# Strassen products for the paired first layers of batches 2 and 3, in an attention-plus-two-MLPs kernel on one Trainium2 core

## The chip, the cores and the metric

One core of one Trainium2 chip. The metric is the device time of one execution in microseconds (us), measured without the profiler; 1371.0 us is the median of three runs before the change. The profile is one further execution, taken with the hardware profiler on; its times are its own. Engines: PE is TensorE (matmuls; PEld are its weight loads), ACT is ScalarE, DVE is VectorE, POOL is GpSimd, SP issues most DMAs.

## The reference

Batch 4, 12 heads, sequence 448, head size 64, so a model width of 768. Attention with capped scores, then an MLP over a normalised input, then a second block that mixes tokens and has an MLP of its own:

```python
scores = cap * np.tanh(scale * q @ k.T / cap); attn = softmax(scores); x = attn @ v     # (4, 448, 768)
xn = (x - mean) / np.sqrt(var + 1e-06) * g_ln
x = x + np.maximum(xn @ w_ch1, 0.0) @ w_ch2                   # w_ch1 768 x 3072: "MLP 1"
u = x + (np.maximum(x.T @ w_tok1, 0.0) @ w_tok2).T            # token mixing, per batch
out = u + np.maximum(u @ w_ch1, 0.0) @ w_ch2                  # w_ch1 768 x 1536: "MLP 2"
```

All data is float32. Each matrix operand is kept as a high and a low part, and a product takes three matmul passes (high-high, low-high, high-low).

## The kernel before

Work is written down as steps; a planner (`Program.emit`) puts the steps of each engine in one fixed order by a key (roughly the time at which a step is due) and by its own estimates of cost. The chip then runs these orders, with semaphores between the engines. So a change in what is written, or in a key, can move any instruction behind it.

Both MLPs are cut into groups of 512 hidden units: six groups in MLP 1 (`NG1`), three in MLP 2 (`NG2`). A group (`mlp`) has a first layer of four row tiles (128 hidden units each) and a second layer of six output tiles. For one batch a first-layer tile is 6 x 3 = 18 matmuls of 128 x 448 (L587) into one PSUM bank; ACT rectifies the bank into the high part (L592) and DVE makes the low part (L593). A second-layer tile is 4 x 3 = 12 matmuls (L608), and DVE adds the bank to the residual `x` (L612). So one group costs one batch 72 + 72 = 144 matmuls. The planner takes a first-layer tile in three parts and a second-layer tile in two, so work of another kind can stand between the parts.

A group runs "paired", for two batches on the same weights, or "solo". Weights were split into high and low parts at first use and kept in DRAM; later uses load them (L296) into three rotating buffers `split`. The last third of the program handles batches 2 and 3:

```python
weave(mlp(groups((2,), 0, n1)))                     # n1 = 6: MLP 1 of batch 2, solo
layer_norm(3)
normalise(3)
weave(mlp(groups((2, 3), n1, NG1 - n1)))            # none, as n1 = NG1
weave(tokens(2, HIDDEN[2]), mlp(groups((3,), 0, n1)), ahead=TOKENS_AHEAD)
weave(tokens(3, HIDDEN[2]), mlp(groups((2,), NG1, n2)), ahead=TOKENS_AHEAD)
weave(mlp(groups((2, 3), NG1 + n2, NG2 - n2), (2,)))
weave(mlp(groups((3,), NG1, n2), (3,)))             # n2 = 2
```

So 16 of the 17 late group runs are solo and one is paired. PSUM has four separate tiles `bank0` to `bank3` of 512 columns, and two tiles `sc0` and `sc1` of two times 512 columns each, which attention uses for its scores, both halves at a time. The MLPs take their banks from a ring; behind attention that ring holds `bank1` to `bank3`.

Of the kernel before, what the change touches and what calls it, by code (L numbers as in the profile page):

```python
# [9 lines left out]
F32 = mybir.dt.float32  # L10
# [9 lines left out]
C = H * D  # L20
# [5 lines left out]
G = 4  # L26
# [60 lines left out]
class Program:  # L87
# [1 line left out]

    FIXED = {"pe": 0.0, "act": 0.19, "dve": 0.08, "pool": 0.15, "dma": 0.3}
    RATE = {"pe": 203e-3 / S, "act": 0.83e-3, "dve": 1.14e-3, "pool": 2.4e-3, "dma": 2.9e-3}
    LATER = {"dma": 3.31}

    def __init__(self):
# [55 lines left out]
def block_kernel(ctx: ExitStack, tc: tile.TileContext, qkv, cap, gln, w1, w2, wt1, wt2, con, out):  # L152
# [10 lines left out]
    def place(name, shape, dtype=F32):  # L163
        return cp.tile([P, *shape], dtype, name=name)

    def boxes(name, n, shape, dtype=F32):
        return [Box(place(f"{name}{i}", shape, dtype)) for i in range(n)]
# [32 lines left out]
    HID = boxes("h", 2 * G, [2, S], F32R)  # L200


    area_t = place("area", [4 * S + QKV + 5 * S])
    ends = [0]

    def area(n):
        ends.append(ends[-1] + n)
        return area_t[:, ends[-2]:ends[-1]]

    own_t = area(4 * S).rearrange("p (e s) -> p e s", e=4)  # L210
# [3 lines left out]
    QK, V = [Box(area(S + 4 * P))], [Box(area(4 * DV).rearrange("p (c d) -> p c d", c=4))]  # L214
    two = [Box(area(S)), Box(area(S))]
    SQ = [Box(area(S))]
    SUM, OTHER = [Box(area(S))], [Box(area(S))]
    TWICE = [Box(OTHER[0].at[:, :CC].rearrange("p (e a d) -> p e a d", e=3, a=2), OTHER)]
    QS, KS = boxes("qs", 1, [2, S], F32R), boxes("ks", 1, [4 * P], F32R)

    VS = boxes("vs", 1, [4, DV + D], F32R)
    EH, EL = boxes("eh", 1, [2, S], F32R), boxes("el", 1, [2, S], F32R)
    M, N = boxes("m", 2, [2, 2, NJ]), boxes("n", 1, [2, 2, NJ])
    rs_t, rm_t = [place(f"rs{i}", [H, NJ]) for i in range(2)], [place(f"rm{i}", [H, NJ]) for i in range(2)]
    RS = [[Box(t[:, 6 * g:6 * g + 6]) for g in range(2)] for t in rs_t]
    RM = [[Box(t[:, 6 * g:6 * g + 6]) for g in range(2)] for t in rm_t]
    R, VA = boxes("r", 1, [2, 32]), boxes("va", 1, [3, 8])
    MEAN, RSTD = boxes("mean", 1, [S]), boxes("rstd", 1, [S])

    BANKS = [Box(pp.tile([P, 512], F32, name=f"bank{i}")) for i in range(4)]  # L230
    SC = [Box(pp.tile([P, 2, 512], F32, name=f"sc{i}")) for i in range(2)]

    def ring(of):
        while True:
            yield from of


    GL, PAIR = Box(gl), Box(pair_r)

# [314 lines left out]
        prog.key += cols * prog.RATE["pe"] * stretch  # L554

    n_tile = 0

    def prepare(g):

# [9 lines left out]
    def mlp(plan, ends=()):  # L569

        nonlocal n_tile
        for n_group, (g, bs) in enumerate(plan):
            final = [b for b in bs if all(b not in o for _, o in plan[n_group + 1:])]
            hid = {b: [] for b in bs}
            hidden = HIDDEN[len(bs) == 1]
            for i in range(G):
                no, row = n_tile, g * G + i
                n_tile += 1
                load(no, w1, row, C)
                w = split_t[no % 3]  # L580
                for b in bs:
                    ph, ht, src = next(main_banks), next(hidden), BIG[b % 2]
                    for part in range(3):
                        def product(part=part, w=w, src=src, ph=ph):
                            for cc in (2 * part, 2 * part + 1):
                                for n, (wi, xi) in enumerate(PASSES):
                                    mm(ph.at[:, :S], w[:, wi, cc * P:(cc + 1) * P], src[cc].at[:, xi],  # L587
                                       start=(cc, n) == (0, 0), stop=(cc, n) == (NCC - 1, 2))

                        need = SPLIT[no % 3][:1] if part == 0 else SPLIT[no % 3][1:] if part == 2 else SPLIT[no % 3]  # L590
                        pe(6 * S, product, [*need, src[2 * part], src[2 * part + 1]], [ph])
                    add("act", S, lambda ht=ht, ph=ph: act(ht.at[:, 0], ph.at[:, :S], AF.Relu), [ph], [ht], early=EVACUATE)  # L592
                    add("dve", S, lambda ht=ht, ph=ph: dve.scalar_tensor_tensor(  # L593
                        ht.at[:, 1], ph.at[:, :S], 0.0, ht.at[:, 0].bitcast(F32), op0=ALU.max, op1=ALU.subtract), [ph], [ht], early=EVACUATE)
                    hid[b].append(ht)
                    yield
            for e in range(NCC):
                no, row = n_tile, g * NCC + e
                n_tile += 1
                load(no, w2, row, G * P)  # L600
                w = split_t[no % 3]
                for b in bs:
                    py, x = next(main_banks), X[b][e]
                    for part in range(2):
                        def product(part=part, w=w, h=hid[b], py=py):
                            for i in (2 * part, 2 * part + 1):
                                for n, (wi, hi) in enumerate(PASSES):
                                    mm(py.at[:, :S], w[:, wi, i * P:(i + 1) * P], h[i].at[:, hi],  # L608
                                       start=(i, n) == (0, 0), stop=(i, n) == (G - 1, 2))

                        pe(6 * S, product, [*SPLIT[no % 3], hid[b][2 * part], hid[b][2 * part + 1]], [py])
                    add("dve", S, lambda x=x, py=py: dve.tensor_tensor(x.at, x.at, py.at[:, :S], op=ALU.add), [py], [x], early=EVACUATE)  # L612
                    if b in ends and b in final:
                        add("dma", S // 2, lambda b=b, e=e, x=x: nc.sync.dma_start(out=out[e, :, b], in_=x.at), [x], ())
                    yield
            if mixing and len(bs) == 2 and n_group >= 1:
                prog.key -= LEAD
                piece(*mixing.pop(0))
                prog.key += LEAD
# [182 lines left out]
```

## Time and profile before

| | |
|---|---|
| runs without the profiler | 1371.0, 1377.17, 1370.46 us, median 1371.0 |
| profiled execution: span from first to last instruction | 4738.7 us (the page gives no other time of this execution) |
| PE busy in it | 4729.0 us, 100% |
| DVE, ACT, POOL busy | 897.2, 624.6, 88.9 us |
| granted TensorE clock, mean | 1.000 (the upper level, 2.4 GHz) |

The profiled execution takes 3.456 times the median of the runs. A busy time is the sum of the instructions' own durations; an engine that is 100% busy leaves no idle time in which another engine's lateness would show.

### The profile page before, as it was taken

Reading aid. Unit: us, or ns where it says so; the run is one execution under the profiler, and the core shown is the slowest. Engines: PE = TensorE matmul, PEld = TensorE weight load, DVE = VectorE, ACT = ScalarE, POOL = GpSimd, SP = SyncE. Lnnn points to the kernel's source line nnn. Section 1 sums busy time; section 2 is a strip of 40 time slices with the busy share of each in tenths; the row PEclk is TensorE's granted clock in tenths of the full one; section 3 lists DMA queues with packets and bytes.
Section 4 is the critical chain, followed back from the end, with each engine's and each line's share of the span. In section 5 each row is a group of like instructions: output and inputs, shape, how many; then the busy total and the mean of one; then the engine's idle time right before and its main releaser. Section 6 shows DMA issues by size and latency. Waiting matters only on the chain.

```text
span 4738.7 us, 17824 instructions
## 1 busy us (share of the span) xinstructions
PE 4729.0 (100%) x6468; PEld 2684.3 (57%) x6468; DVE 897.2 (19%) x1612; ACT 624.6 (13%) x1006; POOL 88.9 (2%) x79
## 2 busy tenths in 40 slices
PE   9999999999999999999999999999999999999999
PEld 2223555555655556665555555555656555656555
DVE  2231222222222222222222221100000000000000
ACT  3321111211121111121111110000000000000000
POOL 1100000000000000000000000000000000000000
DMA  3221122111212111221111211111111111111111
GB/s 105 97 66 39 46 69 67 59 61 64 67 55 67 63 57 41 67 65 61 60 60 51 72 57 53 57 62 58 53 53 44 61 59 60 51 47 42 37 57 58
DMA packets 147095, 281.04 MB, mean 59 GB/s; under 512 B 10816, under 2 KB 79680, under 8 KB 147008
## 3 DMA queue, kind: packets, MB, share of 16 engines
q1 hardware_dynamic: 146432, 279.62, 18.5%
q8 instruction: 51, 0.84, 0.1%
q10 hardware_dynamic: 576, 0.29, 0.0%
q14 instruction: 36, 0.29, 0.0%
HBM read 217.74 MB, written 62.13 MB: 59 GB/s over the span
## 4 chain that ended last, share of the span: by engine, by line
PE 100%; DMA 0%; ACT 0%; DVE 0%; issue 0%
PE bank L587 39%; PE bank L608 39%; PE bank L384 6%; PE sc L363 3%; PE sc L366 3%; PE bank L408 3%; PE bank L663 2%; PE bank L685 2%; PE bank L639 1%; PE bank L466 1%; PE bank L531 0%; PE bank L495 0%; PE bank L511 0%; DMA area<-in_qkv 0%; PE bank L445 0%; PE bank L444 0%
## 5 line engine op out<-in xcount | busy, mean ns | idle before, releaser
L587 PE MATMUL bank<-big,split 128*128 128x448 f32 x2592 | 1898.7, 995 | 1.1 <-ACT big L543 1.1
L608 PE MATMUL bank<-h,split 128*128 128x448 f32 x2592 | 1896.3, 995 | 0.0
L587 PEld LDWEIGHTS bank<-big,split 128*128 128x128 f32 x2592 | 1109.4, 429 | 750.5 <-issue 740.4
L608 PEld LDWEIGHTS bank<-h,split 128*128 128x128 f32 x2592 | 1109.5, 428 | 744.9 <-issue 741.6
L612 DVE TENSOR_TENSOR x<-x,bank 128x448 f32<-128x448 f32 x216 | 134.1, 621 | 1407.4 <-PE bank L608 1407.4
L592 ACT ACTIVATE h<-bank 128x448 fp32r<-128x448 f32 x144 | 78.4, 545 | 1817.5 <-PE bank L587 1817.5
L593 DVE SCALAR_TENSOR_TENSOR h<-bank,h 128x448 fp32r<-128x448 f32 x144 | 89.9, 624 | 1182.2 <-ACT h L592 1182.1
L366 PE MATMUL sc<-qs,ks 128*128 128x448 f32 x192 | 151.5, 994 | 0.0
L384 PE MATMUL bank<-x,area 128*96 128x448 f32 (+1 forms) x88 | 129.3, 1665 | 0.0
L363 PE MATMUL sc<-area 64*128 64x448 f32 x112 | 112.0, 1695 | 5.0 <-DMA area<-in_qkv 5.0
L366 PEld LDWEIGHTS sc<-qs,ks 128*128 128x128 f32 x192 | 82.5, 431 | 57.6 <-issue 57.2
L384 PE MATMUL bank<-x,x 128*96 128x448 f32 (+1 forms) x76 | 112.5, 1675 | 0.0
L685 PE MATMUL bank<-t,h 128*128 128x448 f32 x144 | 108.3, 996 | 0.0
L176 ACT ACTIVATE split<-whole 128x384 fp32r<-128x384 f32 (+1 forms) x96 | 54.0, 564 | 340.2 <-PE bank L608 228.7
L276 ACT ACTIVATE whole<-raw 128x384 f32<-128x384 f32 (+2 forms) x130 | 76.7, 593 | 125.5 <-DVE split L172 107.8
L663 PE MATMUL bank<-big,t 128*128 128x384 f32 x136 | 89.8, 899 | 0.0
L172 DVE TENSOR_TENSOR split<-whole,split 128x384 fp32r<-128x384 f32 (+1 forms) x112 | 68.9, 619 | 108.1 <-ACT split L176 107.7
L408 PE MATMUL bank<-el,vs 128*128 128x448 f32 x96 | 88.6, 989 | 0.0
L685 PEld LDWEIGHTS bank<-t,h 128*128 128x128 f32 x144 | 61.4, 427 | 40.8 <-issue 40.0
L384 PEld LDWEIGHTS bank<-x,area 128*96 128x96 f32 (+1 forms) x88 | 28.5, 347 | 95.4 <-issue 85.5
L279 DVE SCALAR_TENSOR_TENSOR whole<-raw,whole 128x384 int32<-128x384 int32 (+2 forms) x130 | 79.8, 616 | 0.2
L363 PE MATMUL sc<-x 64*128 64x448 f32 x80 | 79.4, 1692 | 0.0
(112 smaller groups left out, 1719.0 us busy)
## 6 DMA issues: line engine op xcount, KB each, us to landing
split<-kept SPq DMA_DIRECT2D x160, 384.0 KB, 3.4
split<-kept SPq DMA_DIRECT2D x120, 512.0 KB, 3.6
raw<-in_w SPq DMA_DIRECT2D x72, 384.0 KB, 3.3
kept<-split SPq DMA_DIRECT2D x72, 384.0 KB, 3.0
raw<-in_w SPq DMA_DIRECT2D x54, 512.0 KB, 3.6
kept<-split SPq DMA_DIRECT2D x54, 512.0 KB, 3.3
area<-in_qkv SPq DMA_DIRECT2D x38, 480.0 KB, 3.5
area<-in_qkv SPq DMA_DIRECT2D x35, 192.0 KB, 2.4
```

Of the source, the lines that this page charges most:

```text
L279: add("dve+", m, lambda: dve.scalar_tensor_tensor(f, hi, -(1 << 31), f, op0=ALU.bitwise_and, op1=ALU.bitwise_or), [r], [w])
L363: mm(sc.at[:, i, :S], k[rows, c * P:(c + 1) * P], q[rows], start=True, stop=True)
L366: mm(sc.at[:, i, :S], ks.at[:, c * P:(c + 1) * P], qs.at[:, j], start=j == 0, stop=j == 1)
L384: mm(po.at[:DV, :S], v.at[:n, c], E[c // 2][0][:n, c % 2], start=c == 0, stop=c == 3)
L408: mm(po.at[:, :S], vs.at[:, c, :P], part.at[:, i], start=c == 0 and part is eh, stop=c == 3)
L587: mm(ph.at[:, :S], w[:, wi, cc * P:(cc + 1) * P], src[cc].at[:, xi], start=(cc, n) == (0, 0), stop=(cc, n) == (NCC - 1, 2))
L592: add("act", S, lambda ht=ht, ph=ph: act(ht.at[:, 0], ph.at[:, :S], AF.Relu), [ph], [ht], early=EVACUATE)
L593: add("dve", S, lambda ht=ht, ph=ph: dve.scalar_tensor_tensor(ht.at[:, 1], ph.at[:, :S], 0.0, ht.at[:, 0].bitcast(F32), op0=ALU.max, op1=A ...
L608: mm(py.at[:, :S], w[:, wi, i * P:(i + 1) * P], h[i].at[:, hi], start=(i, n) == (0, 0), stop=(i, n) == (G - 1, 2))
L612: add("dve", S, lambda x=x, py=py: dve.tensor_tensor(x.at, x.at, py.at[:, :S], op=ALU.add), [py], [x], early=EVACUATE)
L663: mm(pj.at[:, :CC], t1[:, wi, sc * DT + j * P:sc * DT + (j + 1) * P], cols(xs[sc])[:, xi], start=(sc, wi, xi) == (0, 0, 0), stop=(sc, wi) ...
L685: mm(pu.at[:, :S], hT[j].at[:, hi, a:a + P], t2[:, wi, j * S:(j + 1) * S], start=(j, n) == (0, 0), stop=(j, n) == (1, 2))
```

## The change

In a group that is paired for batches 2 and 3, the first layer is computed as Strassen products. The 2 x 2 blocks are: weights, two row tiles by two halves of the width 768; inputs, two halves of the width by two batches. A quad (`quads`, two per group) makes two row tiles for both batches from seven block products of nine matmuls (`times`), where eight such blocks of work stood before. The sums of input blocks `X1` to `X4` are made once per MLP by `sides`, the sums of weight blocks for each quad by `weights`; every sum is split into high and low part by ACT and DVE. DVE adds the products (`plus`) into `TMP` buffers, from which `rectify` makes the hidden tiles. `relay` places the new buffers on tiles that attention and the splitting of weights no longer need. The constants change the division into groups: MLP 1 of batch 2 now runs 3 groups solo, batch 3 runs 1 + 2 solo, 3 are paired; in MLP 2 each batch runs 1 solo and 2 are paired. That is 8 solo and 5 paired group runs. From this point on the ring of banks has eight entries, the four halves of `sc0` and `sc1` and then the four banks.

```diff
-N0, N1, N20, N2 = 1, 6, 1, 2
+N0, N1, N20, N2, N30 = 1, 3, 1, 1, 1
+QUAD_LEAD, SIDES_LATER, SIDES_PACE = 16.0, 20.0, 4.0
...
-    SC = [Box(pp.tile([P, 2, 512], F32, name=f"sc{i}")) for i in range(2)]
+    sc_t = [pp.tile([P, 2, 512], F32, name=f"sc{i}") for i in range(2)]
+    SCB = [Box(t[:, i]) for t in sc_t for i in range(2)]
+    SC = [Box(t, SCB[2 * i:2 * i + 2]) for i, t in enumerate(sc_t)]
...
+    def split(to, src, cols):
+        add("act/dve*+", cols, lambda e: copy(e, to.at[:, 0], src.at), [src], [to])
+        add("dve+", cols, lambda: low(dve, to.at[:, 1], src.at, to.at[:, 0]), [src], [to])
+
+    def join(to, pair, cols):
+        add("dve+/pool+", cols, lambda e: engine_of[e].tensor_tensor(
+            to.at, pair.at[:, 0].bitcast(F32), pair.at[:, 1].bitcast(F32), op=ALU.add), [pair], [to])
+
+    def both(to, a, b, op, cols):
+        add("dve+", cols, lambda: dve.tensor_tensor(to.at, a.at, b.at, op=op), [a, b], [to])
...
+            join(f21, a21, CC)
+            join(f22, a22, CC)
+            both(f22, f21, f22, ALU.add, CC)
+            split(s1, f22, CC)
+            join(f11, a11, CC)
+            both(f21, f11, f21, ALU.subtract, CC)
+            both(f11, f22, f11, ALU.subtract, CC)
+            split(s2, f11, CC)
+            split(a21, f21, CC)
+            join(f12, a12, CC)
+            both(f12, f12, f11, ALU.subtract, CC)
+            split(s4, f12, CC)
...
+        def times(w, x):
+            bank = next(main_banks)
+
+            def product():
+                for c in range(3):
+                    for n, (wi, xi) in enumerate(PASSES):
+                        mm(bank.at[:, :S], w.at[:, wi, c * P:(c + 1) * P], x[c].at[:, xi],
+                           start=(c, n) == (0, 0), stop=(c, n) == (2, 2))
+
+            pe(9 * S, product, [w, *x], [bank])
+            return bank
...
+            p5 = times(s1, X1)
+            p6 = times(s2, X2)
+            plus(c21, p6, c11)
+            plus(c11, p2, c11)
+            h11 = rectify(2, c11)
+            plus(c12, p5, c21)
+            p7 = times(s3, X3)
+            plus(c22, p7, c12)
+            plus(c21, p7, c21)
+            p4 = times(a22, X4)
+            plus(c21, p4, c21)
...
+            if bs == (2, 3):
+                yield from quads(g, hid, hidden)
-            for i in range(G):
+            for i in range(G if bs != (2, 3) else 0):
...
+        main_banks = ring(SCB + BANKS)
+        relay()
+        sides(SIDES_LATER)
+        weave(mlp(groups((3,), 0, N30)))
         weave(mlp(groups((2, 3), n1, NG1 - n1)))
-        weave(tokens(2, HIDDEN[2]), mlp(groups((3,), 0, n1)), ahead=TOKENS_AHEAD)
+        weave(tokens(2, HIDDEN[2]), mlp(groups((3,), N30, n1 - N30)), ahead=TOKENS_AHEAD)
         weave(tokens(3, HIDDEN[2]), mlp(groups((2,), NG1, n2)), ahead=TOKENS_AHEAD)
-        weave(mlp(groups((2, 3), NG1 + n2, NG2 - n2), (2,)))
-        weave(mlp(groups((3,), NG1, n2), (3,)))
+        sides(SIDES_LATER)
+        weave(mlp(groups((3,), NG1, n2)))
+        weave(mlp(groups((2, 3), NG1 + n2, NG2 - n2), (2, 3)))
```

What this does to the orders shows at two places. The first is PE in the second layer of a paired group. Before (the paired group of MLP 2), a tile of batch 2 reads the hidden tiles `h0`, `h2`, `h4`, `h6`, a tile of batch 3 the odd ones, each in a bank of its own; a row's last bracket names the semaphores (DMA queues or engines) that the instruction waits for.

```order
L608 MATMUL bank1_112<-h0_86,split1_78 128x448 [waits DMAHW4_49,DVE_49]
L608 MATMUL bank1_112<-h0_86,split1_78 128x448 x2
L608 MATMUL bank1_112<-h2_88,split1_78 128x448 x3
L608 MATMUL bank1_112<-h4_90,split1_78 128x448 x3
L608 MATMUL bank1_112<-h6_92,split1_78 128x448 x3
L608 MATMUL bank2_113<-h1_87,split1_78 128x448 [waits DVE_49]
L608 MATMUL bank2_113<-h1_87,split1_78 128x448 x2
L608 MATMUL bank2_113<-h3_89,split1_78 128x448 x3
L608 MATMUL bank2_113<-h5_91,split1_78 128x448 x3
L608 MATMUL bank2_113<-h7_93,split1_78 128x448 x3
```

After (first paired group of MLP 1; L770 is the same line, batch 2 reads `h0`, `h1`, `h4`, `h5`), both tiles of one `split` buffer stand in `sc0`: twelve matmuls in its first half, then twelve in its second half.

```order
L770 MATMUL sc0_117<-h0_86,split2_79 128x448 [waits DMAHW0_49]
L770 MATMUL sc0_117<-h0_86,split2_79 128x448 x2
L770 MATMUL sc0_117<-h1_87,split2_79 128x448 x3
L770 MATMUL sc0_117<-h4_90,split2_79 128x448 x3
L770 MATMUL sc0_117<-h5_91,split2_79 128x448 x3
L770 MATMUL sc0_117<-h3_89,split2_79 128x448 x3
L770 MATMUL sc0_117<-h2_88,split2_79 128x448 x3
L770 MATMUL sc0_117<-h7_93,split2_79 128x448 [waits DVE_49]
L770 MATMUL sc0_117<-h7_93,split2_79 128x448 x2
L770 MATMUL sc0_117<-h6_92,split2_79 128x448 x3
```

What moved is a wait. Before, a tile waits at its start, for DVE to have read what stood in the same bank three tiles earlier. After, the second part of the tile in the second half waits for DVE. The awaited instruction is the addition of `sc0`'s first half to `x2`, and that addition waits for PE's first six matmuls into the second half. DVE's order at this place (L774 is L612 of before, L609 is `join`, L613 is `both`):

```order
L774 TENSOR_TENSOR x2_82<-x2_82,bank2_115 128x448 [waits PE_49]
L774 TENSOR_TENSOR x3_83<-x3_83,bank3_116 128x448 [waits PE_49]
L774 TENSOR_TENSOR x2_82<-x2_82,sc0_117 128x448 [waits PE_49]
L774 TENSOR_TENSOR x3_83<-x3_83,sc0_117 128x448 [waits PE_49]
L609 TENSOR_TENSOR late_pair_6982<-split1_78 128x384 [waits DMAHW7_49,DMAHW3_49]
L613 TENSOR_TENSOR v_96<-late_pair_6982,v_96 128x384 [waits DVE_49,Pool_49]
L774 TENSOR_TENSOR x2_82<-x2_82,sc1_118 128x448 [waits PE_49]
```

Here the weight sums of the next quad (L609, L613) have moved between the additions of the second layer.

The second place is PE in the first layer. Before, a row tile takes 18 matmuls for batch 2 (`big0`) and 18 for batch 3 (`big1`):

```order
L587 MATMUL bank2_113<-big0_84,split0_77 128x448 [waits DMAHW0_49]
L587 MATMUL bank2_113<-big0_84,split0_77 128x448 x8
L587 MATMUL bank2_113<-big0_84,split0_77 128x448 [waits DMAHW1_49]
L587 MATMUL bank2_113<-big0_84,split0_77 128x448 x8
L587 MATMUL bank3_114<-big1_85,split0_77 128x448 [waits DVE_49]
L587 MATMUL bank3_114<-big1_85,split0_77 128x448 x17
```

After, products of nine matmuls follow each other, and those on sums (`late_...`, `ksvs`, `eh0`) wait for ACT and DVE, which made the sums:

```order
L673 MATMUL bank3_116<-late_x1_6262,late_qk_6984 128x448 [waits Activation_49]
L673 MATMUL bank3_116<-late_x1_6262,late_qk_6984 128x448 [waits DVE_49]
L673 MATMUL bank3_116<-late_x1_6262,late_qk_6984 128x448 x7
L673 MATMUL sc1_118<-big1_85,ksvs_102 128x448 [waits Activation_49]
L673 MATMUL sc1_118<-big1_85,ksvs_102 128x448 [waits DVE_49]
L673 MATMUL sc1_118<-big1_85,ksvs_102 128x448 x7
L673 MATMUL sc1_118<-big0_84,split0_77 128x448 [waits DMAHW6_49]
L673 MATMUL sc1_118<-big0_84,split0_77 128x448 x8
```

What moved is that the weights no longer come from a DMA alone; sums made on DVE, POOL and ACT stand between the DMA and PE.

## Rows read from the trace of the kernel before

**Rows 1.** The page: span; busy us (share of the span) and instructions per engine.

```profile
span 4738.7 us, 17824 instructions
...
PE 4729.0 (100%) x6468; PEld 2684.3 (57%) x6468; DVE 897.2 (19%) x1612; ACT 624.6 (13%) x1006; POOL 88.9 (2%) x79
```

**Rows 2.** The page: the chain that ended last, shares of the span.

```profile
PE 100%; DMA 0%; ACT 0%; DVE 0%; issue 0%
```

**Rows 3.** Waits on PE, whole span: engine, line, releaser: us in total, times, longest.

```profile
PE sc L363 <- DMA area<-in_qkv: 5.0, 1, 5.0
PE bank L587 <- ACT big L543: 1.1, 1, 1.1
```

**Rows 4.** Chain in order of time, 3000 to 3400 us: start, us, what.

```profile
3056.92 51.67 PE bank L587 x72
3108.59 51.67 PE bank L608 x72
```

**Rows 5.** Stretches of the last part: us, busy per engine (instructions), clock, DMA share, GB/s.

```profile
core 0: us, PE busy (x) PEld busy (x) DVE busy (x) ACT busy (x) POOL busy (x), PEclk, DMA share, GB/s
2500.00:3000.00 500.00, 500.00 (x702) 298.13 (x701) 118.66 (x205) 63.93 (x92) 9.06 (x7) 1.00 0.18 57
3000.00:3500.00 500.00, 500.00 (x711) 299.56 (x710) 34.94 (x57) 15.11 (x29) 0.00 (x0) 1.00 0.19 59
4000.00:4500.00 500.00, 500.00 (x715) 300.72 (x714) 40.80 (x67) 19.01 (x36) 0.00 (x0) 1.00 0.14 45
```

**Rows 6.** Instructions in order of time, 3000 to 3030 us: start, us, engine, line, operation.

```profile
3004.78 26.15 PE L608 MATMUL bank<-h,split 128*128 128x448 f32 x36
...
3005.19 0.55 ACT L592 ACTIVATE h<-bank 128x448 fp32r<-128x448 f32 x1 [10.51 <-PE bank L587]
...
3005.77 0.62 DVE L593 SCALAR_TENSOR_TENSOR h<-bank,h 128x448 fp32r<-128x448 f32 x1 [10.43 <-ACT h L592]
...
3013.80 0.62 DVE L612 TENSOR_TENSOR x<-x,bank 128x448 f32<-128x448 f32 x1 [7.40 <-PE bank L608]
...
3022.46 0.62 DVE L612 TENSOR_TENSOR x<-x,bank 128x448 f32<-128x448 f32 x1 [8.04 <-PE bank L608]
```

**Rows 7.** Instructions in order of time, 570 to 600 us.

```profile
584.10 1.96 ACT L543 ACTIVATE big<-area 128x448 fp32r<-128x448 f32 x4
...
584.72 8.87 PE L587 MATMUL bank<-big,split 128*128 128x448 f32 x12 [1.10 <-ACT big L543]
```

**Rows 8.** Groups by line and shape, DVE, ACT, POOL: busy us, mean ns of one, idle before.

```profile
L612 DVE TENSOR_TENSOR x<-x,bank 128x448 f32<-128x448 f32 x216 | 134.1, 621 | 1407.4 <-PE bank L608 1407.4
L484 DVE TENSOR_TENSOR area<-x,mean 128x448 f32<-128x448 f32 x36 | 21.2, 618 | 20.6 <-ACT mean L496 20.6
L172 DVE TENSOR_TENSOR split<-whole,split 128x384 fp32r<-128x384 f32 x64 | 36.0, 569 | 56.6 <-ACT split L176 56.6
L176 ACT ACTIVATE split<-whole 128x384 fp32r<-128x384 f32 x55 | 28.3, 518 | 108.6 <-PE bank L608 47.9 <-issue 45.5 <-DVE whole L280 15.1
L543 ACT ACTIVATE big<-area 128x448 fp32r<-128x448 f32 x24 | 12.6, 568 | 32.6 <-DVE area L541 32.6
L172 POOL TENSOR_TENSOR split<-whole,split 128x384 fp32r<-128x384 f32 x8 | 8.0, 1005 | 44.1 <-ACT split L176 24.1 <-DVE split L178 20.0
```

**Rows 9.** The page: DMA queue of SP, and issues (KB each, us to landing).

```profile
q1 hardware_dynamic: 146432, 279.62, 18.5%
...
split<-kept SPq DMA_DIRECT2D x160, 384.0 KB, 3.4
split<-kept SPq DMA_DIRECT2D x120, 512.0 KB, 3.6
```

More of the change, by code (lines that the diff above doesn't have):

```diff
@@ L161, in block_kernel, with place @@
     dp = ctx.enter_context(tc.tile_pool(name="dp", bufs=1, space=bass.MemoryType.DRAM))
-    def place(name, shape, dtype=F32):
-        return cp.tile([P, *shape], dtype, name=name)
+    def place(name, shape, dtype=F32, tag=""):
+        return cp.tile([P, *shape], dtype, name=name, tag=tag or name)
     def boxes(name, n, shape, dtype=F32):
@@ L200, in block_kernel @@
     HID = boxes("h", 2 * G, [2, S], F32R)
[L203 to L210, printed above, removed]
+    own_t = place("own", [4, S])
     own = [Box(own_t[:, i]) for i in range(4)]
@@ L213, in block_kernel @@
     OWN = [Box(own_t[:, 2 * i:2 * i + 2], own[2 * i:2 * i + 2]) for i in range(2)]
[L214 to L217, printed above, removed]
+    QK = boxes("qk", 1, [S + 4 * P])
+    v_t, two_t = place("v", [4 * DV]), place("two", [2, S])
+    V = [Box(v_t.rearrange("p (c d) -> p c d", c=4))]
+    two = [Box(two_t[:, i]) for i in range(2)]
+    SQ, SUM, OTHER = boxes("sq", 1, [S]), boxes("sum", 1, [S]), boxes("other", 1, [S])
     TWICE = [Box(OTHER[0].at[:, :CC].rearrange("p (e a d) -> p e a d", e=3, a=2), OTHER)]
-    QS, KS = boxes("qs", 1, [2, S], F32R), boxes("ks", 1, [4 * P], F32R)
-    VS = boxes("vs", 1, [4, DV + D], F32R)
+    QS = boxes("qs", 1, [2, S], F32R)
+    ksvs_t = place("ksvs", [4 * P + 4 * (DV + D)], F32R)
+    KS, VS = [Box(ksvs_t[:, :4 * P])], [Box(ksvs_t[:, 4 * P:].rearrange("p (c d) -> p c d", c=4))]
     EH, EL = boxes("eh", 1, [2, S], F32R), boxes("el", 1, [2, S], F32R)
     M, N = boxes("m", 2, [2, 2, NJ]), boxes("n", 1, [2, 2, NJ])
-    rs_t, rm_t = [place(f"rs{i}", [H, NJ]) for i in range(2)], [place(f"rm{i}", [H, NJ]) for i in range(2)]
+    r_t = place("rsm", [4 * H * NJ])
+    rs_t, rm_t = [[r_t[:, i * H * NJ:(i + 1) * H * NJ].rearrange("p (h j) -> p h j", h=H) for i in two_of] for two_of in ((0, 1), (2, 3))]
     RS = [[Box(t[:, 6 * g:6 * g + 6]) for g in range(2)] for t in rs_t]
@@ L235, in ring, with halves_of, relay, later @@
             yield from of
+    X1, X2, X3, X4 = LATE = [[Box(), Box(), Box()] for _ in range(4)]
+    WF, WS = [Box() for _ in range(4)], [Box() for _ in range(3)]
+    TMP = [Box(r_t[:, :S], [box for of in RS + RM for box in of]), *SQ, *SUM, *OTHER, *MEAN, *RSTD]
+    def halves_of(t):
+        return t.rearrange("p (a s) -> p a s", a=2)
+    def relay():
+        def later(old, boxes, fill):
+            old = [p for box in old for p in box.parts]
+            add("place", 0, fill, (), old + boxes)
+        def fill_x(b):
+            t = place(f"late_x{b}", [3, 2, S], F32R, tag=f"x{b}")
+            for i in range(3):
+                LATE[b][i].at = t[:, i]
+        for b in range(2):
+            later(X[b], LATE[b], lambda b=b: fill_x(b))
+        def fill_raw():
+            for i in range(3):
+                X3[i].at = place(f"late_raw{i}", [2, S], F32R, tag=f"raw{i}")
+            X4[2].at = QS[0].at
+        later(RAW + QS, [*X3, X4[2]], fill_raw)
+        def fill_own():
+            t = place("late_own", [2, 2, S], F32R, tag="own")
+            for i in range(2):
+                X4[i].at = t[:, i]
+        later(own, X4[:2], fill_own)
+        def fill_weights():
+            for i in range(2):
+                WF[i].at = place(f"late_whole{i}", [CC], tag=f"whole{i}")
+            WF[2].at = place("late_pair", [CC], tag="pair_r")
+            WF[3].at = v_t
+            WS[0].at = halves_of(place("late_two", [2 * CC], F32R, tag="two"))
+            WS[1].at = halves_of(place("late_qk", [2 * CC], F32R, tag="qk0"))
+            WS[2].at = halves_of(ksvs_t[:, :2 * CC])
+        later([*WHOLE, PAIR, *V, *two, *QK, *KS, *VS], [*WF, *WS], fill_weights)
+        for box in (*EH, *EL):
+            WS.append(Box(box.at[:, :, :CC], [box]))
     GL, PAIR = Box(gl), Box(pair_r)
@@ new lines, in sides @@
+    def sides(later):
+        t0 = prog.key
+        for c in range(3):
+            prog.key = t0 + later + c * SIDES_PACE
+            f12, f22, f11, f21 = (next(tmps) for _ in range(4))
+            for to, pair in ((f11, BIG[0][c]), (f12, BIG[1][c]), (f22, BIG[1][c + 3]), (f21, BIG[0][c + 3])):
+                join(to, pair, S)
+            both(f11, f12, f11, ALU.subtract, S)
+            split(X1[c], f11, S)
+            both(f12, f22, f12, ALU.subtract, S)
+            split(X3[c], f12, S)
+            both(f22, f22, f11, ALU.subtract, S)
+            split(X2[c], f22, S)
+            both(f21, f21, f22, ALU.subtract, S)
+            split(X4[c], f21, S)
+        prog.key = t0
@@ new lines, in quads, with weights, plus, rectify @@
+    def quads(g, hid, hidden):
+        nonlocal n_tile
+        pieces = []
+        s = [split_t[(n_tile + k) % 3] for k in range(3)]
+        sb = [SPLIT[(n_tile + k) % 3] for k in range(3)]
+        halves = [Box(s[k][:, :, i * CC:(i + 1) * CC], [sb[k][i]]) for k in range(3) for i in range(2)]
+        n_tile += 3
+        def weights(q):
+            a21, a22, a11, a12 = halves[:4] if q == 0 else WS[3:] + halves[4:]
+            row = g * G + 2 * q
+            t0 = prog.key
+            prog.key = t0 - QUAD_LEAD
+            for box, r, at in ((a22, row + 1, CC), (a21, row + 1, 0), (a11, row, 0), (a12, row, CC)):
+                kb = kept[C, r, at]
+                add("dma", CC, lambda box=box, kb=kb: nc.sync.dma_start(out=box.at.bitcast(F32), in_=kb.at), [kb], [box])
+            f11, f12, f21, f22 = WF
+            s1, s2, s4 = WS[:3]
+            join(f21, a21, CC)
[10 more added lines that the diff above has]
+            split(s4, f12, CC)
+            prog.key = t0
+            return a11, a12, a22, s1, s2, a21, s4
+        def times(w, x):
+            bank = next(main_banks)
+            def product():
+                for c in range(3):
+                    for n, (wi, xi) in enumerate(PASSES):
[3 more added lines that the diff above has]
+            return bank
+        def plus(to, bank, t):
+            add("dve", S, lambda: dve.tensor_tensor(to.at, bank.at[:, :S], t.at, op=ALU.add), [bank, t], [to])
+        def rectify(b, src):
+            ht = next(hidden)
+            add("act", S, lambda: act(ht.at[:, 0], src.at, AF.Relu), [src], [ht], early=EVACUATE)
+            add("dve+", S, lambda: dve.scalar_tensor_tensor(
+                ht.at[:, 1], src.at, 0.0, ht.at[:, 0].bitcast(F32), op0=ALU.max, op1=ALU.subtract), [src], [ht], early=EVACUATE)
+            return ht
+        b11, b21, b22 = BIG[0][:3], BIG[0][3:], BIG[1][3:]
+        for q in range(2):
+            a11, a12, a22, s1, s2, s3, s4 = weights(q)
+            c11, c21, c12, c22 = (next(tmps) for _ in range(4))
+            p1 = times(a11, b11)
+            add("act", S, lambda c11=c11, p1=p1: act(c11.at, p1.at[:, :S], AF.Copy), [p1], [c11])
+            p2 = times(a12, b21)
+            yield
+            p5 = times(s1, X1)
[9 more added lines that the diff above has]
+            plus(c21, p4, c21)
+            h21 = rectify(2, c21)
+            h22 = rectify(3, c22)
+            yield
+            p3 = times(s4, b22)
+            plus(c12, p3, c12)
+            h12 = rectify(3, c12)
+            hid[2] += [h11, h21]
+            hid[3] += [h12, h22]
+            yield
```

5 lines of the change are left out of this document (3 added, 2 removed).

## The prediction

> **What bounds the kernel now.** I read the page's engine line first [rows 1], then the chain that ended last [rows 2], then PE's waits [rows 3]. PE is busy for 4729.0 of 4738.7 us, the whole chain is PE, and in all PE waited twice, 5.0 us for the first load and 1.1 us for ACT. So in the profiled execution the time is the number of matmuls times their pitch. In the pure MLP stretch, 72 matmuls take 51.67 us [rows 4], a pitch of 717.6 ns. The granted clock is 1.00 in every stretch that I read [rows 5], which is the upper level, and both idle times left it there.
>
> The profiled execution is no scale model of a run: a run takes 1371.0 us. If all but the two idle times (6.1 us) shrinks alike, the factor is (1371.0 - 6.1) / (4738.7 - 6.1) = 0.2884, and a matmul has a pitch of 207 ns in a run. That is a ceiling. If a twentieth of the run were idle time that the profile's slow PE hides, the pitch would be 197 ns. What ACT, DVE and a DMA take is a duration in its own right, and I use it unscaled. So everything beside PE weighs 3.5 times as much in a run as the page shows: DVE's 897.2 us [rows 1] are 19% of the span but 65% of a run. I make the sum in the profiled time and in the run's time, and the forecast is for the run. About 0.5% (6.9 us, 1364.1 to 1377.9) is what a measurement of this kernel can tell from no change.
>
> **What the change removes.** Two first-layer row tiles for two batches are eight blocks of nine matmuls; a quad makes seven products. Five paired groups with two quads each save 10 x 9 = 90 matmuls. All else on PE keeps its count. In the profiled time that is 90 x 0.7176 = 64.6 us, in a run 90 x 0.207 = 18.6 us (17.7 at the pitch of 197 ns).
>
> It also removes loads: 13 late group runs in place of 17, four times eight 384 KB and six 512 KB loads. PE waited for no such load [rows 3], so I cost that at nothing. The cover in a run: a solo second-layer tile takes 12 x 0.207 = 2.48 us; with three buffers a load has two tiles, 4.97 us, and needs 3.6 us to land [rows 9] behind 0.41 us from the last matmul (below). Some 0.9 us are to spare.
>
> **What it adds beside PE.** Per quad DVE gets seven additions out of PSUM and four low parts at 0.62 us, four sums and four low parts of weights at 0.57 us [rows 8]: 11.4 us. POOL gets up to four joins at 1.0 us. PE needs 63 x 0.207 = 13.0 us for the quad. Behind two quads stands their group's second layer, 144 x 0.207 = 29.8 us of PE, in which DVE has only 12 additions, 7.4 us. So a paired group is 2 x 13.0 + 29.8 = 55.9 us of PE, 30.2 us of DVE and 8 us of POOL. The weight sums are due 16 us ahead (`QUAD_LEAD`) and stand among the second layer's additions in DVE's order, as the change's part shows. `sides` is 12 times join, sum and split on each of two occasions: at most 36 x 0.62 = 22 us of DVE beside a solo group of 29.8 us. I cost all this at nothing. If the cover were gone, it would be the second rival below.
>
> At this place the trace and a rule of the Trainium skill have to be weighed. The row: POOL's subtraction of 384 columns takes 1005 ns over eight instances and DVE's 569 ns [rows 8]; none of these rows shows one engine blocked by the other for a whole instruction. The Trainium skill, page "SBUF — State Buffer", section "Who interferes with whom", says that a DVE instruction with two SBUF inputs and a GpSimd instruction that reads SBUF exclude each other, and that the later one blocks until the first is done. By that rule the joins would come on top of DVE's time; by the row they run beside it. No run here shows which.
>
> **What it adds on PE: waits.** This decides. The ring now begins with the four halves of `sc0` and `sc1`, and the built program treats the two halves of one `sc` as one tile. DVE's addition of the first half waits for PE's first part into the second half, and the second part waits for that addition. Before, the ring held three tiles, and the wait at a tile's start was for the reader of the tile three back; it cost nothing [rows 3].
>
> The price of one such wait, from the last matmul before it to the next: PE to DVE, 12 matmuls from 3004.78 us at 0.7176 end at 3013.39, DVE starts at 3013.80 [rows 6], 0.41 us; the addition, 0.62 us; to PE, the first L543 ends at 584.10 + 0.57 = 584.67 [rows 7, 8] and PE, which waited for it, starts at 584.72, 0.05 us. Together 1.08 us. It does not shrink with PE. Through ACT alone, at 0.55 us [rows 6], it is 1.01 us; through ACT and then DVE, with 0.03 us between them [rows 6], 1.66 us.
>
> Counted along the changed order, with the awaited instructions: 13 second-layer tiles and two transposes between their parts wait for an addition with nothing to cover it, 15 x 1.08 = 16.2 us; solo first-layer tiles wait five times, twice for ACT, twice for DVE behind ACT, once for both, 2 x 1.01 + 2 x 1.08 + 1.66 = 5.8 us; three more waits are partly covered by other matmuls, together between nothing and 3.2 us, and I take 1.0. In quads the same dependency only delays DVE: a product is one step of nine matmuls, so no part of it waits. The sum is 23.0 us. Bounds: DVE's 0.62 us alone for 20 waits, 12.4 us; and 20 times 1.08 plus one more addition queued ahead on DVE, 0.62, plus 3.2, 37 us. I take 23.0, since rows 6 show DVE idle when such an addition comes.
>
> **Sum.** Profiled: 4738.7 - 64.6 + 23.0 = 4697.1 us. Run: 1371.0 - 18.6 + 23.0 = 1375.4 us. The Strassen saving is real and the waits eat it.
>
> **Rivals.**
> *The waits are cheap.* PE's weight loads run ahead of matmuls, and PEld is busy for only 57% [rows 1]; if PE and DVE overlapped more of the chain than I think, the price would fall towards DVE's 0.62 us or nothing. For it: the drain of 0.41 us is read in an execution whose matmuls are slow. Against: the awaited addition reads the very bank whose matmuls must have drained, and PE started only 0.05 us behind ACT's end in the one such case. Time: 1371.0 - 18.6 + 12.4 = 1364.8 us, and 1352.4 us if they cost nothing. It counts as faster from 0.58 us per wait.
>
> *The operands of the quads come late: slower.* Place: the first product of a quad on a sum (`late_two`, `late_qk`, `ksvs`). If joins on POOL block DVE for their whole length and nothing of it fits beside the second layer, a quad takes DVE 11.4 + 4.0 = 15.4 us against PE's 13.0, 2.4 us for each of ten quads, 24 us: 1375.4 + 24 = 1399 us. From 0.25 us per quad it decides the verdict. For it: no row of before has DVE that full beside POOL; in the last part DVE was busy 34.94 of 500 us [rows 5], which is some 24% of a run's time there. Against: the averages above, 38 of 55.9 us even with the block.
>
> *Loads were late in solo groups, unseen by the profile.* A solo group moves 6.3 MB. By [rows 9] the 16 engines need 0.185 x 4738.7 / 279.62 = 3.1 us per MB, 19.7 of the group's 29.8 us. If each second-layer tile were 0.2 us late, eight solo runs fewer would give back 8 x 6 x 0.2 = 10 us: 1366 us. Against: the 0.9 us to spare.
>
> **How the numbers follow.** The likeliest, the waits at about their price, has 0.62; its own range is 1370 to 1381 us, 18 to 29 us of waits. The waits cheap: 0.13. Late operands: 0.18. Late loads: 0.07. Slower by over 0.5% is all of the late operands and a bit over a quarter of the likeliest: 0.35. Faster by over 0.5%: most of the two cases that give time back: 0.15. Within: 0.50. The range is 1360 to 1392 us: it leaves out half of the cheap waits and nearly half of the late operands.
>
> **What the changed profile would show.** A span near 4697 us; PE's waits with a new entry of some 15 times 1.1 us, second layer on `sc` behind DVE's additions, and ACT and DVE entries for the solo first layers on `sc`; no wait on products; matmuls of an unchanged pitch, 90 fewer; DVE some 120 us busier. Wrong would be: no PE waits on `sc` (then the run is near 1352), waits at the quads' products (near 1399), or a clock below 1.00.

## Result and the profile after

The changed kernel runs in 1380.38 us (median of 8 runs, 1377.91 to 1384.70), the kernel before in 1372.51 us (8 runs, 1370.46 to 1377.17). The ratio is 1.0051 with a 95% interval of 1.0035 to 1.0068: slower by 7.9 us. The interval lies above 1, so the kernel became slower, by just the 0.5% that the prediction took as the least that can be told from no change. The forecast was 1375.4 us in a range of 1360 to 1392.

The page of the changed kernel: span, busy us per engine (share, instructions), the SP queue, and the chain by engine and by line.

```profile
span 1377.7 us, 17881 instructions
...
PE 1339.9 (97%) x6378; PEld 1154.8 (84%) x6378; DVE 1031.8 (75%) x1819; ACT 658.5 (48%) x1081; POOL 161.2 (12%) x133
...
q1 hardware_dynamic: 131200, 254.45, 56.8%
...
PE 90%; DVE 4%; ACT 4%; DMA 1%; issue 1%; ACTq 0%; DVEq 0%
PE bank L770 30%; PE bank L749 25%; PE sc L770 8%; PE bank L673 5%; PE sc L673 5%; PE sc L749 3%; PE sc L411 3%; PE bank L429 3%; PE bank L453 2%; PE bank L825 2%; PE bank L847 1%; ACT x L414 1%; PE sc L408 1%; ACT x L415 1%; DVE x L774 1%; DVE m L419 1%
```

The span is 1377.7 us, close to a run, where [rows 1] have 4738.7. The profiled execution of [rows 1] had PE at 717.6 ns per matmul; this one has it at 203. A second profile of the unchanged kernel (label b0_before, below) also ran at 203 ns, so the pace belongs to that one execution and not to the kernel; why it was so slow stayed open. All comparisons from here on are with b0_before. Line numbers moved: L749 is L587 of before, L754 and L755 are L592 and L593, L770 is L608, L774 is L612; L673 are the products, L680 their additions (`plus`).

PE's waits in the changed kernel (engine, tile, line, releaser: us in total, times, longest), the whole span:

```profile
PE sc L770 <- DVE x L774: 9.3, 13, 0.7
PE sc L408 <- ACT x L414: 5.1, 7, 1.7
PE sc L408 <- DMA qk<-in_qkv: 4.8, 1, 4.8
PE sc L749 <- DVE h L755: 2.1, 2, 1.4
PE bank L749 <- ACT big L588: 1.8, 2, 1.1
PE sc L801 <- DVE x L774: 1.8, 3, 0.7
...
PE sc L749 <- ACT h L754: 1.3, 2, 0.7
...
PE sc L749 <- DVE h L834: 0.7, 1, 0.7
PE sc L770 <- DVE x L851: 0.7, 1, 0.7
```

The first line is new: 13 times a second-layer tile (L770) in an `sc` waits for DVE's addition L774. So are the L749 and L801 lines on `sc`: first layers of solo groups, and transposes. L408 is attention, early, and has its counterpart before. There is no line for the products L673 at all. The page and the waits of b0_before show the other side:

```profile
span 1371.7 us, 17824 instructions
...
PE 1350.9 (98%) x6468; PEld 1173.9 (86%) x6468; DVE 897.9 (65%) x1612; ACT 619.6 (45%) x1006; POOL 94.4 (7%) x79
```

```profile
PE sc L363 <- DMA area<-in_qkv: 5.1, 1, 5.1
PE sc L363 <- ACT x L369: 3.6, 5, 1.7
PE bank L587 <- ACT big L543: 1.8, 2, 1.1
PE bank L587 <- DVE big L172: 1.7, 2, 1.1
...
PE bank L608 <- DMA split<-kept: 0.5, 1, 0.5
```

The last of these lines is the only wait of PE that this trace lists from 870 us on.

PE is busy 11.0 us less with the change (1350.9 to 1339.9) and yet the span is 6.0 us longer (1371.7 to 1377.7): 17 us went into idle time. One of the places, in the chain of the changed kernel in order of time (start, us, what):

```profile
1026.55 3.66 PE sc L770 x18
1030.21 0.02 issue
1030.24 0.63 DVE x L774
1030.87 0.04 issue
1030.91 5.14 PE sc L770 x24
1036.06 0.02 issue
1036.08 0.63 DVE x L774
1036.71 0.04 issue
```

Twelve matmuls into the first half of an `sc`, six into the second, then PE stops until DVE has added the first half to `x`, then it goes on. The same again 24 matmuls later, at the next tile pair.

To size all of this I read the start of every matmul from 870 us on (the part that the change touches) and added up what lies over the usual 202.7 ns from one start to the next. These sums are my own, worked out from the traces; which of the short gaps are counted moves a row by up to some 2 us, so small differences between rows mean little:

```
kernel           lost from 870 us on   of it, on sc: second layer, first layer, transposes; products anywhere
b0_before          1.8 us              0      0     0     -
changed           24.0 us             14.2    5.5   2.2   0
e1_halves_apart    4.7 us              0.3    0     0     0.8
e3_ring_only      31.6 us             13.5   15.9   0     -
e4_halves_only    94.8 us             39.8    7.2   4.0  37.6
e5_banks_only     23.8 us              0      0     0    16.6
e6_one_between     6.5 us              1.8    0     0     1.0
e7_joins_dve       5.0 us              0.2    0     0     1.4
```

In the changed kernel 14 second-layer gaps and two transposes lose 0.87 to 0.88 us each, and the slot behind each gap loses another 0.1 us. So the account from 870 us on is: 90 matmuls saved at 0.2028 us, -18.2 us; waits, 24.0 - 1.8 = +22.2 us; a mean pitch of 203.3 in place of 202.8 ns over some 2,400 matmuls, +1.4 us. That is +5.4 of the 6.0 us between the two spans. The medians are 7.9 us apart; the other 2 us lie in runs without a trace. These 2 us and the 0.6 us between the spans stay open.

### The profile page after: what moved, and what is told of

Read it like the earlier page. It is cut to its first block, busy times and chain, and to the rows that moved or that the text cites. A ratio compares the mean times of both kernels' runs of the same rounds, so it can differ in the third digit from the quotient of the medians.

```text
span 1377.7 us, 17881 instructions
## 1 busy us (share of the span) xinstructions
PE 1339.9 (97%) x6378; PEld 1154.8 (84%) x6378; DVE 1031.8 (75%) x1819; ACT 658.5 (48%) x1081; POOL 161.2 (12%) x133
## 3 DMA queue, kind: packets, MB, share of 16 engines
q1 hardware_dynamic: 131200, 254.45, 56.8%
## 4 chain that ended last, share of the span: by engine, by line
PE 90%; DVE 4%; ACT 4%; DMA 1%; issue 1%; ACTq 0%; DVEq 0%
PE bank L770 30%; PE bank L749 25%; PE sc L770 8%; PE bank L673 5%; PE sc L673 5%; PE sc L749 3%; PE sc L411 3%; PE bank L429 3%; PE bank L453 2%; PE bank L825 2%; PE bank L847 1%; ACT x L414 1%; PE sc L408 1%; ACT x L415 1%; DVE x L774 1%; DVE m L419 1%
## 5 line engine op out<-in xcount | busy, mean ns | idle before, releaser
L770 PE MATMUL bank<-h,split 128*128 128x448 f32 x2064 | 437.7, 367 | 1.4 <-DVE x L774 1.3
L770 PEld LDWEIGHTS bank<-h,split 128*128 128x128 f32 x2064 | 386.1, 188 | 34.9 <-DVE x L774 2.1
L749 PE MATMUL bank<-big,split 128*128 128x448 f32 x1656 | 354.2, 368 | 3.5 <-ACT big L588 1.8
L749 PEld LDWEIGHTS bank<-big,split 128*128 128x128 f32 x1656 | 310.5, 188 | 33.4 <-ACT big L588 2.9
L774 DVE TENSOR_TENSOR x<-x,bank 128x448 f32<-128x448 f32 x172 | 105.9, 617 | 82.9 <-PE bank L770 81.7
L770 PE MATMUL sc<-h,split 128*128 128x448 f32 x528 | 115.2, 369 | 10.0 <-DVE x L774 9.3
L770 PEld LDWEIGHTS sc<-h,split 128*128 128x128 f32 x528 | 97.7, 188 | 22.9 <-DVE x L774 14.1
L754 ACT ACTIVATE h<-bank 128x448 fp32r<-128x448 f32 x92 | 49.9, 542 | 89.9 <-PE bank L749 89.5
L774 DVE TENSOR_TENSOR x<-x,sc 128x448 f32<-128x448 f32 x44 | 27.0, 620 | 72.7 <-PE sc L770 70.8
L322 ACT ACTIVATE raw<-raw 128x384 int32<-128x384 uint32 (+2 forms) x130 | 77.5, 600 | 0.0
L755 DVE SCALAR_TENSOR_TENSOR h<-bank,h 128x448 fp32r<-128x448 f32 x92 | 56.6, 616 | 26.6 <-ACT h L754 25.6
L325 DVE CUSTOM_DVE_ANT_0 whole<-raw,whole 128x768 uint16<-128x768 uint16 (+2 forms) x116 | 74.2, 642 | 0.0
L323 DVE TENSOR_SCALAR whole<-whole 128x384 int32<-128x384 int32 (+2 forms) x130 | 55.0, 426 | 3.6 <-ACT whole L321 3.2
L419 DVE TRANSPOSE_TENSOR_REDUCE m<-own 128x28 f32<-128x896 f32 x48 | 52.9, 1101 | 4.9 <-ACT own L415 4.9
```

Source lines behind the costliest of these rows:

```text
L322: add("act", m, lambda: act(lo, lo.bitcast(U32), AF.Copy, scale=2.0 ** -29), (), [r])
L325: add("pool+" if ahead else "dve+", m, lambda e: engine_of[e].tensor_tensor(f, f, lo, op=ALU.add), [r], [w])
L419: add("dve", 2 * S, lambda half=half, e=e: dve.tensor_reduce(m.at[:, half].rearrange("p c j -> p (c j)"), e.rearrange("p c (j i) -> p (c j ...
```

## Experiments

**The kernel before, profiled again (b0_before).**

> The kernel before once more, for a profile at the pace of a run: the first one showed TensorE at 717.6 ns per matmul, the changed kernel's shows 203 ns. Both theories expect a span near 1370 us. If the waits on the other half of an sc tile are the whole story, its first two thirds (attention, batches 0 and 1) have the same PE idle time as the changed kernel's, some 17 us in the first 200 us, and its last part has PE idle time near zero. The rival, that the new placement of buffers costs time in attention, expects less PE idle time in its first 200 us than the changed kernel has.

Measured: 1373.45 us, span 1371.7. This is the profile used above. In the first 200 us PE is idle for 16.5 us here and for 17.5 in the changed kernel, which is the direction that the rival expected, by 1.0 us. But the 700th matmul starts at 210.1 us here and at 210.2 us in the changed kernel, and in both the 3900th starts at 853.3 us, so that rival explains none of the difference between the two spans. In e1 and e2 below the 3900th starts at 855.7 and 849.9 us: the part ahead of the change differs by some us from one profiled execution to the next. From the 3900th matmul to the end it is 518.4 us here, 524.5 in the changed kernel and 506.2 in e1.

**The halves of an `sc` kept apart in the ring (e1_halves_apart).** The changed kernel with one line different: the same eight places, in an order in which the two halves of one tile are four places apart.

```diff
-        main_banks = ring(SCB + BANKS)
+        main_banks = ring([box for i in (0, 2, 1, 3) for box in (SCB[i], BANKS[(0, 2, 1, 3).index(i)])])
```

> The changed kernel with the same eight banks in another order: the two halves of an sc tile stand four places apart in the ring, with single banks between; all else, the order of PE's work too, is the same. Theory (waits on the other half): the some 23 waits, 16 us of PE idle time in the changed kernel's trace and up to 20 us counted from the end of the last matmul's slot, go; 1360 to 1364 us. Rival (quads or the regrouping cost the time): no or little change, 1375 to 1381 us.

Measured: 1361.87 us (1361.47 to 1366.05), ratio to the kernel before, which ran in 1374.14 us beside it, 0.9917 (0.9902 to 0.9931). PE's waits from 870 us on, the two longest of the four that are left (the others are 0.3 and 0.2 us):

```profile
PE sc L825 <- DVE x L774: 0.8, 1, 0.8
PE sc L673 <- DMA split<-kept: 0.4, 1, 0.4
```

The waits of L770, L749 and L801 on `sc` are gone, and with them 18.5 us of the medians; the table has 24.0 - 4.7 = 19.3 us. Nothing else was changed, and in the two traces PE, DVE, ACT and POOL do the same instructions in the same order, but for the places they use; so the adjacent halves cost that time. This kernel is also the better one: the Strassen products do pay, by 0.8%.

**Only the regrouping (e2_groups_only).** The changed kernel's groups, buffers and order of groups; first layers by row tiles as before, no quads, and neither the new ring, nor `relay`, nor `sides`.

```diff
-            if bs == (2, 3):
-                yield from quads(g, hid, hidden)
-            for i in range(G if bs != (2, 3) else 0):
+            for i in range(G):
...
-        main_banks = ring(SCB + BANKS)
-        relay()
-        sides(SIDES_LATER)
...
-        sides(SIDES_LATER)
```

> The changed kernel without Strassen: the new division into groups and the new buffers stay, the paired first layers are computed in the old way (90 matmuls more), sides, relay and the ring with the halves are left out, the old ring of three banks stays. Theory (waits on the other half): as before, 1371 to 1374 us. Rival (regrouping, or the buffers placed anew, cost some 10 us that the waits don't explain): 1380 to 1385 us.

Measured: 1374.30 us (1372.36 to 1380.28), ratio 1.0006 (0.9995 to 1.0018). Pairing more groups and with that loading weights less often (254.45 MB on SP's queue, where b0_before moved 279.62) moves nothing. That speaks against the rival by which solo groups had waited for loads, and so do the waits: from 870 us on PE waits for a load once in b0_before, for 0.5 us, and here no wait is listed.

**Only the ring (e3_ring_only).** The kernel before, all its groups and products as they were, with the eight-place ring from the same point on.

```diff
-    SC = [Box(pp.tile([P, 2, 512], F32, name=f"sc{i}")) for i in range(2)]
+    sc_t = [pp.tile([P, 2, 512], F32, name=f"sc{i}") for i in range(2)]
+    SCB = [Box(t[:, i]) for t in sc_t for i in range(2)]
+    SC = [Box(t, SCB[2 * i:2 * i + 2]) for i, t in enumerate(sc_t)]
...
         normalise(3)
+        main_banks = ring(SCB + BANKS)
```

> The kernel before with one part of the change: behind the normalising of batch 3 the ring of eight with adjacent halves. Theory (waits on the other half): 13 second-layer tiles at 0.71 us, eight first-layer tiles that wait through ACT and DVE at 1.3 us, and a few more: 20 to 23 us slower, 1392 to 1396 us. Rival: no change, 1371 to 1374 us.

Measured: 1405.92 us (1405.10 to 1406.96), ratio 1.0231 (1.0217 to 1.0245). The two largest entries of PE's waits (L589 is the first layer, L610 the second):

```profile
PE sc L589 <- DVE h L595: 12.1, 9, 1.4
PE sc L610 <- DVE x L614: 8.6, 12, 0.7
```

More than expected, and by the same mechanism: here all but one group are solo, and a solo first-layer tile waits for ACT and then DVE, nine times, 1.3 to 1.4 us each in the list and some 1.5 us from slot to slot. The spans differ by 1403.5 - 1371.7 = 31.8 us, the lost time by 31.6 - 1.8 = 29.8; a mean pitch of 203.7 for 202.8 ns is the other 2 us. So the ring by itself costs more than the Strassen products save.

**A ring of the halves alone (e4_halves_only).** The changed kernel at a larger dose: four places, in which every tile pair stands in the two halves of one `sc`.

```diff
-        main_banks = ring(SCB + BANKS)
+        main_banks = ring(SCB)
```

> The changed kernel with a ring of the four halves alone, adjacent halves next to each other: the dose is raised. Half of all banks are now second halves, and in the built order about 40 waits have nothing to cover them, against 20. Theory (waits on the other half): at the 0.9 to 1.1 us per wait that the changed kernel's trace shows, and with some more that come from having four places in place of eight, 35 to 50 us slower than the changed kernel, 1415 to 1430 us. Rival (the cost of the waits is a fixed cost of something else in the last part): near 1380 us.

Measured: 1458.18 us (1456.78 to 1459.38), ratio 1.0615 (1.0596 to 1.0633), well above what was expected. PE's waits:

```profile
PE sc L770 <- DVE x L774: 22.3, 31, 0.8
PE sc L673 <- DVE sq L680: 9.7, 5, 4.0
PE sc L673 <- DVE other L680: 5.2, 6, 1.4
```

and windows of ten microseconds around one of the longest waits (us, busy per engine, granted clock, DMA share, GB/s):

```profile
930.00:940.00 10.00, 9.36 (x46) 8.31 (x45) 9.24 (x13) 2.62 (x6) 5.92 (x5) 1.00 0.48 161
940.00:950.00 10.00, 5.05 (x14) 3.70 (x13) 5.83 (x10) 3.18 (x6) 0.67 (x1) 0.65 0.00 0
950.00:960.00 10.00, 9.78 (x41) 8.62 (x40) 4.48 (x8) 1.57 (x3) 0.00 (x0) 0.83 0.32 105
```

The second layer's part went as the dose says: 31 waits for 13. What I had left out is the products: with four places a product finds its place unread by `plus`, up to 4 us at a time; 37.6 us are lost there in all. Around the two longest of these waits, 3.58 and 4.02 us, the granted clock fell, and what the slower matmuls cost behind them is part of the lost time.

**A ring of the four single banks (e5_banks_only).** The changed kernel with no halves, but four places in place of eight.

```diff
-        main_banks = ring(SCB + BANKS)
+        main_banks = ring(BANKS)
```

> The changed kernel with a ring of the four single banks, no halves at all. No wait on another half is left; but a quad holds up to four products that DVE has not yet read. If only the shared tile matters, this is as fast as with the halves apart, 1360 to 1364 us. If the eight places matter too, products wait for DVE's reading of the bank four places back, and it lies between, 1365 to 1378 us.

Measured: 1383.71 us (1382.33 to 1384.12), ratio 1.0071 (1.0054 to 1.0088), above the 1365 to 1378 us that were expected. PE's waits:

```profile
PE bank L673 <- DVE sq L680: 5.6, 2, 3.2
...
PE bank L673 <- DMA split<-kept: 3.8, 2, 2.3
...
PE bank L673 <- DVE other L680: 1.4, 2, 0.7
```

From 870 us on there is no wait on an `sc`, and now there are waits at the products, two of them for loads. So the eight places are needed: leaving the halves out trades 22 us of one wait for as much elsewhere, most of it at the products. One such place in e5's order of time (start, us, engine, line):

```profile
933.47 1.36 DVE L613 TENSOR_TENSOR v<-late_pair,v 128x384 f32<-128x384 f32 x1
...
938.40 0.61 DVE L680 TENSOR_TENSOR sq<-bank,rsm 128x448 f32<-128x448 f32 x1
...
939.06 3.49 PE L673 MATMUL bank<-big,split 128*128 128x448 f32 x9 [3.23 <-DVE sq L680]
```

DVE is in the weight sums of the next quad (L613 at 1.36 us), only then comes the addition L680 that frees the bank, and PE waits 3.23 us for it. e4 and e5 together say that places for the quads and distance between the halves are two separate needs, and e1 meets both.

**One bank between the halves (e6_one_between).** Eight places, halves of a tile two places apart:

```diff
-        main_banks = ring(SCB + BANKS)
+        main_banks = ring([box for pair in zip(SCB, BANKS) for box in pair])
```

> As with the halves apart, but with only one single bank between the two halves of a tile: twelve matmuls, 2.4 us, as cover for a chain of about 1 us. Theory: a wait is free as soon as one tile's matmuls cover it, so 1361 to 1365 us. If the chain is longer than the trace shows, it lies clearly above, 1368 us or more.

Measured: 1362.11 us (1360.49 to 1367.96), ratio 0.9926 (0.9906 to 0.9946), the same as e1 within the intervals. Twelve matmuls of another tile between the halves are 2.4 us of cover for a wait of 0.88 us. One wait of this kind is left: at 1197.7 us L770 waits 0.7 us for L774.

**All joins on DVE (e7_joins_dve).** e1 with `join` taken from POOL and given to DVE.

```diff
-        add("dve+/pool+", cols, lambda e: engine_of[e].tensor_tensor(
+        add("dve+", cols, lambda e="dve": engine_of[e].tensor_tensor(
```

> The kernel with the halves apart, with all joins on DVE in place of POOL or DVE. If joins on POOL hold up DVE by locking it out, this is faster or the same, 1358 to 1363 us; if POOL takes load off DVE that counts, the quads' operands come late and it is 3 to 10 us slower, 1365 to 1372 us; if operands have slack either way, no change, 1360 to 1364 us.

Measured: 1362.65 us (1361.25 to 1364.22), ratio 0.9921 (0.9906 to 0.9936), the same as e1. That the operands of the quads have slack is shown from both sides: the time does not depend on which engine the joins stand on. But the page moved: DVE has 56 instructions more than in e1 (1875 for 1819) and is busy no longer (1031.0 for 1032.9 us). What the joins on POOL do to DVE shows in one row, by line and shape, of the sum `v` of two blocks (engine, operation, tile, count: ns min/median/max, first and last start). First the changed kernel, joins on POOL:

```profile
L613 DVE TENSOR_TENSOR v<-late_pair,v x10: 558/1365/1417, 930.0 to 1322.7; 128x384 f32<-128x384 f32 x10
```

and e7, joins on DVE:

```profile
L613 DVE TENSOR_TENSOR v<-late_pair,v x10: 550/556/559, 923.5 to 1305.8; 128x384 f32<-128x384 f32 x10
```

In the order of time of the changed kernel, one of these beside POOL (start, us, engine, line):

```profile
933.90 1.38 DVE L613 TENSOR_TENSOR late_whole<-late_whole,late_whole 128x384 f32<-128x384 f32 x1
935.32 1.25 DVE L173 TENSOR_TENSOR late_qk<-late_whole,late_qk 128x384 fp32r<-128x384 f32 x1
936.50 0.54 DVE L173 TENSOR_TENSOR ksvs<-late_whole,ksvs 128x384 fp32r<-128x384 f32 x1
...
933.52 1.34 POOL L609 TENSOR_TENSOR v<-el 128x384 f32<-128x384 f32 x1 [1.62 <-ACT split L177]
934.83 1.33 POOL L609 TENSOR_TENSOR late_pair<-eh 128x384 f32<-128x384 f32 x1
```

The first two of these DVE instructions, both with two SBUF inputs, started while a join ran and took 1.38 and 1.25 us; each ended some 0.4 us after that join. The third started with no join running and took 0.54 us. By the Trainium skill, page "SBUF — State Buffer", section "Who interferes with whom", the two exclude each other and the later one blocks; these rows agree.

## Why the prediction was right, point by point

**The bound.** Right. PE is 97% busy and 90% of the chain, so matmuls saved and waits added both count in full. The profiled execution was no scale model, as said: DVE is busy for 897.9 us in b0_before where [rows 1] have 897.2, while PE's time is less than a third. The pitch in a run was forecast a little too high: it is 203 ns, not 207. The forecast let all of PE's time shrink alike, and it did not: 4729.0 us of busy PE in [rows 1] scale by 203 / 717.6 to 1338 us, and b0_before has 1351, 13 us more, which was not looked into. Another 11 us are idle time of PE that the slow PE had hidden (span less busy is 20.8 us for 9.7), in attention and at the first layers (L363 and L587 in b0_before's waits).

**The saving.** 90 matmuls, 18.2 us for 18.6. e1 shows it with the waits gone: 1374.14 - 1361.87 = 12.3 us, which is 18.2 less 2.9 us of lost time (4.7 - 1.8) and some 2 us of a slower pitch (203.6 for 202.8 ns); 1 us stays open.

**The waits.** Mechanism and places right: e1 takes the adjacency away and the time goes, e3 adds the ring alone and the time comes. The count was right too, 14 gaps in the second layer and two transposes for 13 and two. The price per wait was too high: 0.88 us for 1.08. The term of 0.41 us from PE to DVE was read in the execution with 717.6 ns per matmul. At a run's pace the slot of the last matmul ends some 0.18 us before that matmul does (its start at 1029.83, its end at 1030.21, a pitch of 0.20), so DVE starts 0.21 us behind the slot, and 0.21 + 0.63 + 0.04 = 0.88. The 0.1 us lost in the slot behind each gap, which I had not foreseen, gives half of that back. Solo first layers cost 5.5 us for 5.8. The sum is 22.2 us for 23.0.

**What was costed at nothing.** Right with eight places: no wait of a product for DVE, ACT or POOL is listed (nor in e7), and there is no gain from fewer loads (e2). Two details were off. DVE became 134 us busier (1031.8 - 897.9) and not some 120. Joins on POOL stretch its sums: e7, with 56 instructions more on DVE, is no busier there. So of the two readings of a join on POOL that the prediction left open, the runs show the one by which it comes on top of DVE's time. And the cover that hid it is not only DVE's idle time in the second layer: e5 shows that it takes eight places as well. There the late work of DVE reaches PE, and it does so at a product's place and not at the first product on a sum, where the second rival had put it.

**Waits cheap.** Refuted: 0.88 us is above the 0.58 at which this case would have begun. **Late operands.** Refuted in this kernel by the missing lines for L673 and by e7. **Late loads.** e2 shows no sign of them, and b0_before lists one wait for a load in this part, 0.5 us, where this case had wanted some 10 us.

**A clock below 1.00,** named as a sign of being wrong, was seen in the mean, 0.996, but as much in b0_before: in both it is 0.97 over the first 200 us and 1.00 in the two stretches behind, so it has no part in the difference.

**The profiled span** of 4697 us was not met, because the profile after ran at a run's pace. For the run, -18.2 + 22.2 = +4.0 where +4.4 was forecast; the rest, up to the measured 7.9, is the slower pitch of 1.4 us and some 2.5 us that no trace explains. So the mechanism and its two terms held. That their sum came so close is in part luck: the price per wait was 0.2 us too high, and half of that came back by a loss that was not foreseen.

## What to carry to other kernels

When a ring of PSUM places is made longer with parts of one tile, put other tiles between the parts: neighbours make PE wait for the reader of the first part in the middle of the second, 0.88 us each time, and one tile between them hides nearly all of it (e6). Count such waits in the built order before trusting a saving in matmuls, since some 20 of them ate 90 matmuls here. And a change that saves work and adds a wait should be split in two runs, one for each, because their sum of 0.5% told nothing of either.

## What was not expected of the hardware

One profiled execution of the kernel before had a matmul pitch of 717.6 ns and another 203 ns; the granted clock was 1.00 and 0.996. No run here shows why.

The mean pitch of the 448-column matmuls in the last part differs by kernel and profile from 202.8 ns (b0_before) to 205.8 ns (the profile of e6, whose 1366.99 us is 5 us above that kernel's median); some 2,400 matmuls at 2.2 ns more than e1's 203.6 are 5 us. Nearly all single distances lie between 199 and 207 ns in all of them, and only their mix changes. What sets the mix was not tried.

In e4 the granted clock was 0.65 and 0.83 in the two windows shown, behind a wait of PE of 3.58 us at the end of a stretch at 1.00; nine matmuls at 944.02 us took 3.73 us where nine at 938.42 took 2.02. The clock went to the lower of the two levels, 1.2 GHz, and came back to 1.00 by 960 us. The same was seen at the wait of 4.02 us (0.77 and 0.72 from 1320 to 1340 us), and e5 has 0.94 and 0.89 in the two windows around its wait of 3.23 us, and 0.96 and 0.87 from 1264 to 1284 us, behind a wait of 2.4 us. In the changed kernel, whose waits in this part are 1.4 us at most, no window of ten microseconds from 870 us on is below 1.00 but the last.
